# A step later, a buffer of its own, free banks ahead: three edits in a layered matmul kernel of attention and two feed-forward blocks

## The chip, the cores and the metric

The kernel runs on one core of one Trainium2 chip. The metric is the device time of one execution in microseconds (us). TensorE multiplies matrices into PSUM; VectorE and ScalarE read and write both PSUM and SBUF; GpSimd works on SBUF alone here; SyncE (SP) issues nearly all DMAs, in order. Each engine works through its own queue in order, and waits at an instruction whose operands or buffers are not ready.

## The reference

Three computations follow one another on fp32 data:

```python
out[:, :, sl] = intra + inter            # retention attention, 2 x 8 heads, 768 positions
p = domain_probs / (domain_probs.sum(-1, keepdims=True) + 1e-09)
for e in range(E):                       # mixture, 1536 tokens, 4 experts, 512 -> 1024 -> 512
    h = np.maximum(x @ w1[e], 0.0)
    out += p[:, e:e + 1] * (h @ w2[e])
h = x @ w_in                             # last block, 512 -> 2048 -> 512
g = h * (1.0 / (1.0 + np.exp(-h)))
return (g @ w_out).astype(np.float32)
```

## The kernel before, in words

**Split operands.** Every fp32 operand of a matmul is split in two parts: ScalarE copies it rounded (the high part, type fp32r), and VectorE or GpSimd subtracts that from the original (the low part). `split` does both. A product is then three matmuls: high by high, low by high, high by low.

**Four stages.** The tokens are three groups of 512. The first stage does attention for all tokens and the mixture for the first group (`gemm1`, `gemm2`, phase "a"). The second does the mixture for the other two groups together (phase "c"): seven products of halves replace eight (`pair_step`), with sums of weight quarters as left operands and sums of input quarters as right ones. The third stage (phase "b") is the last block for the first group, in 16 steps of `gemm1` and `gemm2`. The fourth (phase "d") is the last block for the other two groups, again by seven products, in both layers (`pair7` for the first layer, `down7` for the second).

**Third stage.** A step `i` runs `gemm1` of column block `i` (12 matmuls into one of four banks), the gate (ScalarE sigmoid `sg`, VectorE product, ScalarE copy `hhi`, VectorE `hlo`), and `gemm2` of block `i - 2` (12 matmuls). Every second step also needs the next weights. In an even step `split_up` makes the up weights `ua`, `ub` (ScalarE and GpSimd), and `left_out` prepares weights for the fourth stage: `left_sums` adds four quarters on GpSimd into the tile `us`, ScalarE copies its high part into `uc` (line 693), and GpSimd subtracts in place (line 694). In an odd step the parts are stored to DRAM (`wu`; `left_kept` for the split weights, line 706, and the stored function for the sums, line 700) and `split_down` makes the down weights `dh`, `dl` (ScalarE and VectorE). `combine` sums and splits the right operands for the fourth stage: a difference on VectorE (line 634), a copy on ScalarE (line 626), a subtraction on VectorE at the beginning of the next step (line 627, run by `flush`). `load(0)` and `load(1)` issue the next raw up and down weights (lines 118 and 123); each has two buffers, and the load waits until the readers of the older one are done.

**Into the fourth stage.** `left_in` loads the split weights and sums of pair 0 back from `wu` (line 711), and `left_in2` the others (line 716).

**Fourth stage.** `pair7` computes seven products into four banks `x`, `y`, `z`, `v` by the list `plan`: each entry names a product, what is emitted after it (`then`), and how many fillers follow, with a second list (`later`) after the first filler. The four banks change roles from pair to pair (`roles`). A `filler` takes a waiting second-layer block out of `fill`, and `unit` runs what is due; `after(n, fn)` makes a function due in n units. `operand` has ScalarE copy the high part (`ohi`, line 919) and returns the subtraction of the low part (`olo`, line 921). `down7(g, m, d)` is one block of six matmuls for product `ROUND[m]` and half `d`, in one of four banks `po0` to `po3` in turn. After the last two pairs (`g` = 3), the blocks of products 1, 5, 6 and 2 begin from an accumulator that ScalarE copies into the bank first (line 959), and `sums7` adds the finished blocks to other accumulators; `store` writes results out.

The order of emission is the order in each engine's queue (the schedule is written out by hand).

Of the kernel before, what the change touches and what calls it, by code (L numbers as in the profile page):

```python
# [7 lines left out]
F32 = mybir.dt.float32  # L8
F32R = mybir.dt.float32r
U32 = mybir.dt.uint32  # L10
AF = mybir.ActivationFunctionType
ALU = mybir.AluOpType
# [3 lines left out]
P = 128  # L16
# [22 lines left out]
def kernel(  # L39
# [97 lines left out]
    def load(j, n=1):  # L137
        for _ in range(n):
            if nxt[j] < len(seq[j]):
                ph, i, src = seq[j][nxt[j]]  # L140
                nxt[j] += 1
                (load_up, load_down)[j](src, i, (ph, i))
# [541 lines left out]
    def left_out(i):  # L684

        key = ("b", i)
        left_sums(key)
        low = sum_t.pop(key)
        high = leftp.tile([P, 2, 2, HW], F32R, tag="uc", name="uc").rearrange(
            "p a b n -> p (a b) n"  # L690
        )
        load(0)
        nc.scalar.activation(out=high, in_=low, func=AF.Copy)
        nc.gpsimd.tensor_tensor(
            out=low.bitcast(F32R), in0=low, in1=high.bitcast(F32), op=ALU.subtract
        )

        def stores():
            for n, t in enumerate((high.bitcast(F32), low)):
                nc.sync.dma_start(out=wu[i][:, n, 4:], in_=t)  # L700

        return stores

    def left_kept(i):
        for n, t in enumerate(up_t["b", i]):
# [18 lines left out]
    def after(n, fn):  # L724
        due.append((clock[0] + n, fn))
# [199 lines left out]
    def vadd(out, a, b, op=ALU.add, eng=nc.vector):  # L925
        eng.tensor_tensor(out=out, in0=a, in1=b, op=op)

    def acc_tile(r, d):
        if (r, d) not in acc7:
            if r in (2, 4):  # L930
                if "d" not in acc_t:
                    acc_t["d"] = accp.tile([P, KD, TW], F32, tag="acc", name="acc")
                acc7[r, d] = acc_t["d"][:, r - 2 + d]
            else:
                acc7[r, d] = tmp["d"].tile([P, TW], F32, tag=f"a{r}{d}", name=f"a{r}{d}")
        return acc7[r, d]
# [4 lines left out]

    blocks = [0]

    def down7(g, m, d, part=slice(0, TW)):

        q = 7 * g + m
        r = ROUND[m]
        po = psum.tile([P, TW], F32, tag=f"po{blocks[0] % 4}", name="po")
        blocks[0] += 1
        ops = []  # L950
        for s in range(2):
            whi, wlo = (dw_t[q][:, s, k, d * P:(d + 1) * P] for k in range(2))
            hhi, hlo = op_t[2 * g + s, r]
            ops += [(whi, hhi), (wlo, hhi), (whi, hlo)]
        a = acc_tile(r, d)
        last = g == NV // 2 - 1
        begun = last and r in (1, 5, 6, 2)
        if begun:
            nc.scalar.activation(out=po, in_=a, func=AF.Copy)
        for j, (w, h) in enumerate(ops):  # L960
            nc.tensor.matmul(  # L961
                po[:, part],
                lhsT=w,
                rhs=h[:, part],
                start=(j == 0 and not begun),
                stop=(j == len(ops) - 1),
                skip_group_check=begun,
            )

        def evacuate7():  # L970
            if begun:
                sums7(r, d, po)
            elif g == 0:
                nc.scalar.activation(out=a, in_=po, func=AF.Copy)
            else:
                vadd(a[:, part], po[:, part], a[:, part])
                if last and r == 7:
                    vadd(acc7[4, d], acc7[4, d], a, eng=nc.gpsimd)
                elif last and r == 4:
                    store(a, 2 + d, 0, part)  # L980

        due.append((clock[0] + 1, evacuate7))
        if d == 1:
            for when, fn in jobs7.pop(q, ()):
                after(when, fn)

    def sums7(r, d, po):

        a = {n: acc7[n, d] for n in ROUND}
        if r == 2:  # L990
            nc.scalar.activation(out=a[2], in_=po, func=AF.Copy)
            store(a[2], d, 0)
            return
        for n in {1: (6, 2), 5: (3, 7), 6: (4, 3, 7)}[r]:
            vadd(a[n], po, a[n])
        if r == 6:
            store(a[3], d, 1)
            store(a[7], 2 + d, 1)

# [19 lines left out]
    def pair7(i, prepare):  # L1019

        key = ("d", i)
        order = roles[0]
        x, y, z, v = (psum.tile([P, TW], F32, tag=f"ps{order[r]}", name=r) for r in "xyzv")
        roles[0] = {"x": order["z"], "y": order["x"], "z": order["v"], "v": order["y"]}
        s, low, sig = {}, {}, {}

# [10 lines left out]
        def high(r, c, eng=nc.vector):  # L1037
            low[r] = operand(i, r, c, eng)

        def times(name, c, to):  # L1040
            vadd(to, c, sig[name], ALU.mult)

        def minus(to, a, b):
            vadd(to, a, b, ALU.subtract)
# [24 lines left out]
                1,  # L1069
                [  # L1070
                    lambda: times("x", x, x),
                    lambda: high(1, x),
                    lambda: minus(sig["z"], sig["z"], x),
                ],
            ),
            (
                (4, y, False),
                [
                    lambda: low[1](),
                    lambda: minus(v, v, sig["z"]),  # L1080
                    lambda: high(5, sig["z"], nc.gpsimd),
                    lambda: low[5](),
                    lambda: high(6, v),
                    lambda: vadd(y, y, s[1]),
                    lambda: gated("y", y),
                ],
                2,
                [
# [20 lines left out]
                    for fn in later:  # L1109
                        fn()  # L1110

        def rest():
            minus(y, sig["y"], v)
            high(4, y)

        after(1, rest)
        after(2, lambda: low[4]())

    def jobs_for(key, following):

# [17 lines left out]
    with tc.manual_schedule():  # L1138
# [167 lines left out]
        tmp["sums"] = pool(sums, "sums2", side="right")  # L1306
        split_up(("b", 1), False)
        split_down(("b", 0), nc.vector)
        mixing, stores = [], []
        for i in range(nb):  # L1310
            flush()
            gemm1("b", i)
            unit()
            if i < 2:
                for _ in range(KD):
                    filler()
            elif i < nb - 2:
                gemm2("b", i - 2)
            if i % 2:
                for n in ([0, 1] if i == 1 else [i // 2 + 1]):  # L1320
                    if n < NV:
                        left_kept(n)
                stores.pop()()
                if i < nb - 1:
                    split_down(("b", (i + 1) // 2), nc.vector)
            else:
                if 2 <= i < nb - 2:
                    split_up(("b", i // 2 + 1), False)
                elif i == nb - 2:
                    left_in(0)  # L1330
                stores.append(left_out(i // 2))
            if i == 2:
                mixing = combine(acc_t["c", 0], acc_t["c", 1])
            elif i > 2:
                for job in mixing[i - 3:i - 2]:
                    job()
# [80 lines left out]
```

## Time and profile before

| what | value |
|---|---|
| median of 3 runs | 845.1 us (844.4 to 847.1) |
| profiled execution, its own time | 846.49 us |
| its span, first to last instruction | 844.7 us |
| TensorE matmuls busy | 806.8 us (96%) |
| VectorE / ScalarE / GpSimd busy | 546.7 / 351.6 / 493.0 us |
| mean granted TensorE clock | 0.98 of full speed |
| DMA, mean over the span | 145 GB/s |

The busy shares are means over stages with different limits. Matmuls are pipelined, so that the ends of their records are modelled. In rows of a timeline the columns are: start, duration, engine, line, operation, output and input tiles with their shapes, count, and in brackets the idle time of the engine before and what ended it. A row of waits has the waiting engine and line, the one waited for, the total, the number of times and the longest.

### The profile page before, as it was taken

The numbers are of one execution on the slowest core, as the hardware profiler recorded it, in microseconds if no ns is written. First come the engines' busy times: TensorE is split into PE (matmuls) and PEld (weight loads), VectorE is DVE, ScalarE is ACT, GpSimd is POOL, SyncE is SP. The second block draws the span as 40 slices with busy tenths as digits, with TensorE's granted clock in tenths as the row PEclk, the third lists the DMA queues.
The fourth block names the chain that finished last, engine by engine and source line by source line (L and its number), as shares of the span: only waits on it lengthen the run. The fifth ranks groups of instructions, "written<-read, shape, count | busy, mean of one in ns | idle before, by whom it ended". The sixth has DMA issues, their size and how long they took to land.

```text
span 844.7 us, 11026 instructions
## 1 busy us (share of the span) xinstructions
PE 806.8 (96%) x4084; PEld 660.4 (78%) x4084; DVE 546.7 (65%) x785; ACT 351.6 (42%) x602; POOL 493.0 (58%) x420
## 2 busy tenths in 40 slices
PE   8999999999999999999999999998886699999977
PEld 8888888888888888888888888886564577888766
DVE  6346586766685777777777776735335365577775
ACT  3433333343553333333333333433344367645552
POOL 3846654545675666666666667643554558675761
PEclk9999999999999999999999999999798799999999
DMA  7867768533342232232222211167455644251402
GB/s 290 308 209 242 252 225 272 184 119 122 125 134 82 97 112 87 88 113 88 91 97 98 74 52 63 55 223 264 156 169 229 225 136 139 88 180 45 162 0 100
DMA packets 39480, 122.41 MB, mean 145 GB/s; under 512 B 4434, under 2 KB 4738, under 8 KB 39426
## 3 DMA queue, kind: packets, MB, share of 16 engines
q1 hardware_dynamic: 39424, 121.70, 42.1%
q8 instruction: 32, 0.52, 0.3%
q14 instruction: 22, 0.18, 0.1%
q10 hardware_dynamic: 2, 0.00, 0.0%
HBM read 93.35 MB, written 28.34 MB: 144 GB/s over the span
## 4 chain that ended last, share of the span: by engine, by line
PE 84%; issue 4%; POOL 4%; DVE 4%; DMA 2%; ACT 2%; SPq 0%; POOLq 0%; ACTq 0%; DVEq 0%
PE po L795 21%; PE ph L532 13%; PE po L589 13%; PE y L746 11%; PE z L746 7%; PE x L746 7%; PE po L961 6%; PE s L408 2%; DMA u<-wd 1%; PE xps L447 1%; POOL ub L146 1%; POOL us L668 1%; ACT ohi L919 1%; DVE olo L921 1%; DMA ub<-wu 1%
## 5 line engine op out<-in xcount | busy, mean ns | idle before, releaser
L146 POOL TENSOR_TENSOR ub<-u,ua 128x1024 fp32r<-128x1024 f32 (+2 forms) x41 | 68.0, 1660 | 114.0 <-ACT ua L145 106.7
L795 PE MATMUL po<-hhi,dh 128*128 128x512 f32 x256 | 99.6, 389 | 0.0
L795 PE MATMUL po<-hhi,dl 128*128 128x512 f32 x256 | 99.6, 389 | 0.0
L795 PE MATMUL po<-hlo,dh 128*128 128x512 f32 x256 | 99.6, 389 | 0.0
L809 DVE TENSOR_TENSOR acc<-po,acc 128x512 f32<-128x512 f32 x120 | 79.5, 683 | 28.7 <-PE po L795 28.7
L146 POOL TENSOR_TENSOR dl<-d,dh 128x1024 fp32r<-128x1024 f32 (+1 forms) x33 | 77.0, 2334 | 12.4 <-ACT dh L145 12.4
L559 ACT ACTIVATE hhi<-ph 128x512 fp32r<-128x512 f32 x40 | 23.9, 598 | 118.0 <-DVE ph L553 85.8
L763 POOL TENSOR_TENSOR s<-s,s 128x512 f32<-128x512 f32 x32 | 48.8, 1526 | 30.9 <-ACT s L758 30.9
L532 PE MATMUL ph<-xhi,ua 128*128 128x512 f32 (+1 forms) x208 | 55.8, 391 | 9.1 <-ACT ua L145 8.4
L589 PE MATMUL po<-hhi,dh 128*128 128x512 f32 (+1 forms) x208 | 58.8, 387 | 2.2 <-ACT hhi L559 2.2
L532 PE MATMUL ph<-xhi,ub 128*128 128x512 f32 (+1 forms) x208 | 55.7, 391 | 4.4 <-POOL ub L146 4.0
L146 POOL TENSOR_TENSOR uc<-u,uc 128x512 fp32r<-128x512 f32 x16 | 20.6, 1288 | 66.9 <-ACT uc L145 66.9
L589 PE MATMUL po<-hhi,dl 128*128 128x512 f32 (+1 forms) x208 | 56.0, 373 | 0.0
L589 PE MATMUL po<-hlo,dh 128*128 128x512 f32 (+1 forms) x208 | 55.9, 372 | 0.0
L795 PEld LDWEIGHTS po<-hlo,dh 128*128 128x128 f32 x256 | 48.0, 188 | 10.0
L795 PEld LDWEIGHTS po<-hhi,dl 128*128 128x128 f32 x256 | 48.1, 188 | 10.0
L795 PEld LDWEIGHTS po<-hhi,dh 128*128 128x128 f32 x256 | 48.0, 188 | 9.9
L532 PE MATMUL ph<-xlo,ua 128*128 128x512 f32 (+1 forms) x208 | 54.7, 386 | 0.0
L532 PEld LDWEIGHTS ph<-xhi,ua 128*128 128x128 f32 x208 | 37.5, 192 | 18.6 <-ACT ua L145 10.1
L145 ACT ACTIVATE dh<-d 128x1024 fp32r<-128x1024 f32 (+2 forms) x56 | 47.0, 854 | 7.8 <-PE po L795 3.5
L532 PEld LDWEIGHTS ph<-xhi,ub 128*128 128x128 f32 x208 | 38.8, 197 | 14.1 <-POOL ub L146 6.3
L589 PEld LDWEIGHTS po<-hhi,dh 128*128 128x128 f32 x208 | 38.3, 194 | 10.9 <-ACT hhi L559 3.2
(215 smaller groups left out, 1966.4 us busy)
## 6 DMA issues: line engine op xcount, KB each, us to landing
u<-wts SPq DMA_DIRECT2D x32, 512.0 KB, 3.4
d<-wts SPq DMA_DIRECT2D x32, 512.0 KB, 3.4
words<-wts SPq DMA_DIRECT2D x32, 512.0 KB, 4.8
wd<-dec SPq DMA_DIRECT2D x32, 256.0 KB, 2.8
d<-wd SPq DMA_DIRECT2D x16, 512.0 KB, 3.6
qkt<-qk SPq DMA_DIRECT2D x12, 512.0 KB, 4.5
kvt<-kv SPq DMA_DIRECT2D x10, 512.0 KB, 4.6
ua<-wu SPq DMA_DIRECT2D x8, 640.0 KB, 5.9
```

Of the source, the lines that this page charges most:

```text
L145: nc.scalar.activation(out=hi, in_=src, func=AF.Copy)
L146: eng.tensor_tensor(out=lo, in0=src, in1=hi.bitcast(F32), op=ALU.subtract)
L408: nc.tensor.matmul(s[t, p // n][:, p % n], lhsT=qkt[r, 1, p], rhs=qkt[r, 0, p], start=True, stop=True,)
L447: nc.tensor.matmul(at, lhsT=kvt[:, 1, 2 * p + t], rhs=box[t][p], start=(c == 0), stop=(c == 0 or p >= 2),)
L532: nc.tensor.matmul(pt[:, :n], lhsT=w, rhs=x[:, k, o:o + n], start=(j == 0), stop=(j == len(ops) - 1),)
L559: nc.scalar.activation(out=hi, in_=pt, func=AF.Copy)
L589: nc.tensor.matmul(po_t[d][:, o:o + n], lhsT=w[:, d * P:(d + 1) * P], rhs=h[:, :n], start=(begin and j == 0), stop=(last and j == 2), skip ...
L746: nc.tensor.matmul(to, lhsT=a[:, k * P:(k + 1) * P], rhs=b[:, k], start=(first and j == 0), stop=(j == len(ops) - 1), skip_group_check=not ...
L763: nc.gpsimd.tensor_tensor(out=t, in0=a, in1=b, op=ALU.add)
L795: nc.tensor.matmul(po, lhsT=w, rhs=h, start=(j == 0), stop=(j == len(ops) - 1))
L809: nc.vector.tensor_tensor(out=a, in0=po, in1=a, op=ALU.add)
L961: nc.tensor.matmul(po[:, part], lhsT=w, rhs=h[:, part], start=(j == 0 and not begun), stop=(j == len(ops) - 1), skip_group_check=begun,)
```

## The change

`left_out` now emits the sums alone, ahead of `split_up`, and gives back two functions. The first, called in the next (odd) step, issues the load, makes the high part in `uc` and the low part in a tile of its own, `low`. The second, called after `split_down`, issues the two stores. In the last group of `down7` each block has a bank by the table `FINAL`; some are banks of the first layer. The copies of accumulators are emitted ahead by `begin7`: for product 1 when blocks (3, 1) and (7, 0) are issued, for 5 when the block of product 3 in the same half has been added, and for 6 and 2 when product 1 has been added. In `pair7` the subtraction from `sig["z"]` goes ahead of the copy `high(1, x)`, three more entries go from the list after product 4 to the one after product 2, two subtractions of low parts go behind the gate, and the last subtraction and copy are emitted at once instead of a unit later.

```diff
--- before.py
+++ after.py
@@ -685,21 +685,22 @@
 
         key = ("b", i)
         left_sums(key)
-        low = sum_t.pop(key)
-        high = leftp.tile([P, 2, 2, HW], F32R, tag="uc", name="uc").rearrange(
-            "p a b n -> p (a b) n"
-        )
-        load(0)
-        nc.scalar.activation(out=high, in_=low, func=AF.Copy)
-        nc.gpsimd.tensor_tensor(
-            out=low.bitcast(F32R), in0=low, in1=high.bitcast(F32), op=ALU.subtract
-        )
-
-        def stores():
-            for n, t in enumerate((high.bitcast(F32), low)):
-                nc.sync.dma_start(out=wu[i][:, n, 4:], in_=t)
-
-        return stores
+        src = sum_t.pop(key)
+
+        def halves():
+            load(0)
+            high = leftp.tile([P, 2, 2, HW], F32R, tag="uc", name="uc").rearrange(
+                "p a b n -> p (a b) n"
+            )
+            low = tmp["sums"].tile([P, 4, HW], F32R, tag="low", name="low")
+            split(nc.gpsimd, high, low, src)
+            return high, low
+
+        def stores(tiles):
+            for n, t in enumerate(tiles):
+                nc.sync.dma_start(out=wu[i][:, n, 4:], in_=t.bitcast(F32))
+
+        return halves, stores
 
     def left_kept(i):
         for n, t in enumerate(up_t["b", i]):
@@ -941,34 +942,49 @@
 
     blocks = [0]
 
+    FINAL = {3: "23", 7: "01", 1: "zx", 5: "23", 6: "01", 2: "vy", 4: "zx"}
+    begun = {}
+
+    def block_bank(last, r, d, more):
+        if last:
+            which = "2" if more else FINAL[r][d]
+            tag = f"ps{roles[1][which]}" if which in "xyzv" else f"po{which}"
+        else:
+            tag = f"po{blocks[0] % 4}"
+            blocks[0] += 1
+        return psum.tile([P, TW], F32, tag=tag, name="po")
+
+    def begin7(r, d):
+        begun[r, d] = po = block_bank(True, r, d, False)
+        nc.scalar.activation(out=po, in_=acc_tile(r, d), func=AF.Copy)
+
     def down7(g, m, d, part=slice(0, TW)):
 
         q = 7 * g + m
         r = ROUND[m]
-        po = psum.tile([P, TW], F32, tag=f"po{blocks[0] % 4}", name="po")
-        blocks[0] += 1
+        last = g == NV // 2 - 1
+        if last and (r, d) in ((3, 1), (7, 0)):
+            begin7(1, int(r == 7))
+        on = begun.pop((r, d), None)
+        po = block_bank(last, r, d, part.start > 0) if on is None else on
         ops = []
         for s in range(2):
             whi, wlo = (dw_t[q][:, s, k, d * P:(d + 1) * P] for k in range(2))
             hhi, hlo = op_t[2 * g + s, r]
             ops += [(whi, hhi), (wlo, hhi), (whi, hlo)]
-        a = acc_tile(r, d)
-        last = g == NV // 2 - 1
-        begun = last and r in (1, 5, 6, 2)
-        if begun:
-            nc.scalar.activation(out=po, in_=a, func=AF.Copy)
         for j, (w, h) in enumerate(ops):
             nc.tensor.matmul(
                 po[:, part],
                 lhsT=w,
                 rhs=h[:, part],
-                start=(j == 0 and not begun),
+                start=(j == 0 and on is None),
                 stop=(j == len(ops) - 1),
-                skip_group_check=begun,
+                skip_group_check=on is not None,
             )
+        a = acc_tile(r, d)
 
         def evacuate7():
-            if begun:
+            if on is not None:
                 sums7(r, d, po)
             elif g == 0:
                 nc.scalar.activation(out=a, in_=po, func=AF.Copy)
@@ -976,6 +992,8 @@
                 vadd(a[:, part], po[:, part], a[:, part])
                 if last and r == 7:
                     vadd(acc7[4, d], acc7[4, d], a, eng=nc.gpsimd)
+                elif last and r == 3:
+                    begin7(5, d)
                 elif last and r == 4:
                     store(a, 2 + d, 0, part)
 
@@ -993,7 +1011,10 @@
             return
         for n in {1: (6, 2), 5: (3, 7), 6: (4, 3, 7)}[r]:
             vadd(a[n], po, a[n])
-        if r == 6:
+        if r == 1:
+            begin7(6, d)
+            begin7(2, d)
+        elif r == 6:
             store(a[3], d, 1)
             store(a[7], 2 + d, 1)
 
@@ -1021,6 +1042,7 @@
         key = ("d", i)
         order = roles[0]
         x, y, z, v = (psum.tile([P, TW], F32, tag=f"ps{order[r]}", name=r) for r in "xyzv")
+        roles[1:] = [order]
         roles[0] = {"x": order["z"], "y": order["x"], "z": order["v"], "v": order["y"]}
         s, low, sig = {}, {}, {}
 
@@ -1069,20 +1091,20 @@
                 1,
                 [
                     lambda: times("x", x, x),
+                    lambda: minus(sig["z"], sig["z"], x),
                     lambda: high(1, x),
-                    lambda: minus(sig["z"], sig["z"], x),
+                    lambda: minus(v, v, sig["z"]),
+                    lambda: high(5, sig["z"], nc.gpsimd),
+                    lambda: high(6, v),
                 ],
             ),
             (
                 (4, y, False),
                 [
-                    lambda: low[1](),
-                    lambda: minus(v, v, sig["z"]),
-                    lambda: high(5, sig["z"], nc.gpsimd),
-                    lambda: low[5](),
-                    lambda: high(6, v),
                     lambda: vadd(y, y, s[1]),
                     lambda: gated("y", y),
+                    lambda: low[1](),
+                    lambda: low[5](),
                 ],
                 2,
                 [
@@ -1109,12 +1131,9 @@
                     for fn in later:
                         fn()
 
-        def rest():
-            minus(y, sig["y"], v)
-            high(4, y)
-
-        after(1, rest)
-        after(2, lambda: low[4]())
+        minus(y, sig["y"], v)
+        high(4, y)
+        after(1, lambda: low[4]())
 
     def jobs_for(key, following):
 
@@ -1306,7 +1325,7 @@
         tmp["sums"] = pool(sums, "sums2", side="right")
         split_up(("b", 1), False)
         split_down(("b", 0), nc.vector)
-        mixing, stores = [], []
+        mixing = []
         for i in range(nb):
             flush()
             gemm1("b", i)
@@ -1317,18 +1336,20 @@
             elif i < nb - 2:
                 gemm2("b", i - 2)
             if i % 2:
+                halves, stores = left
+                tiles = halves()
                 for n in ([0, 1] if i == 1 else [i // 2 + 1]):
                     if n < NV:
                         left_kept(n)
-                stores.pop()()
                 if i < nb - 1:
                     split_down(("b", (i + 1) // 2), nc.vector)
+                stores(tiles)
             else:
+                left = left_out(i // 2)
                 if 2 <= i < nb - 2:
                     split_up(("b", i // 2 + 1), False)
                 elif i == nb - 2:
                     left_in(0)
-                stores.append(left_out(i // 2))
             if i == 2:
                 mixing = combine(acc_t["c", 0], acc_t["c", 1])
             elif i > 2:
```

## Rows read from the trace of the kernel before

**Rows 1.** Waits of TensorE from 590 us to the end

```profile
PE ph L532 <- ACT ua L145: 8.4, 4, 2.5
PE po L961 <- ACT po L959: 6.0, 2, 4.8
PE ph L532 <- POOL ub L146: 4.0, 4, 1.2
PE z L746 <- DVE y L926: 2.0, 4, 0.9
```

**Rows 2.** Timeline of SP and of TensorE, 655 to 662 us

```profile
655.72 0.32 SPq L123 DMA_DIRECT2D d<-wd  x1
...
661.33 1.19 PE L746 MATMUL x<-hi,ua 128*128 128x512 f32 x2 [9.08 <-DMA ua<-wu]
```

**Rows 3.** Timeline of TensorE, third stage: passes of `gemm1`

```profile
562.83 1.07 PE L532 MATMUL ph<-xlo,ua 128*128 128x512 f32 x4
...
571.90 1.07 PE L532 MATMUL ph<-xhi,ua 128*128 128x512 f32 x4
...
577.34 1.07 PE L532 MATMUL ph<-xhi,ua 128*128 128x512 f32 x4
...
644.74 2.07 PE L532 MATMUL ph<-xhi,ub 128*128 128x512 f32 x4 [1.23 <-POOL ub L146]
```

**Rows 4.** Timeline of ScalarE, third stage, one turn of two steps

```profile
607.74 1.05 ACT L145 ACTIVATE ua<-u 128x1024 fp32r<-128x1024 f32 x1
614.12 1.06 ACT L693 ACTIVATE uc<-us 128x1024 fp32r<-128x1024 f32 x1 [5.34 <-POOL us L668]
615.09 1.04 ACT L626 ACTIVATE hi<-sum 128x1024 fp32r<-128x1024 f32 x1
...
619.38 0.60 ACT L559 ACTIVATE hhi<-ph 128x512 fp32r<-128x512 f32 x1 [2.76 <-DVE ph L566]
619.87 1.05 ACT L145 ACTIVATE dh<-d 128x1024 fp32r<-128x1024 f32 x1
...
623.96 0.60 ACT L559 ACTIVATE hhi<-ph 128x512 fp32r<-128x512 f32 x1 [2.55 <-DVE ph L566]
```

**Rows 5.** Timeline of VectorE, the same turn, and at 655 us

```profile
616.16 2.57 DVE L627 TENSOR_TENSOR lo<-sum,hi 128x1024 fp32r<-128x1024 f32 x1 [7.59 <-ACT hi L626]
...
620.95 1.23 DVE L146 TENSOR_TENSOR dl<-d,dh 128x1024 fp32r<-128x1024 f32 x1 [0.25 <-ACT dh L145]
622.09 1.22 DVE L634 TENSOR_TENSOR sum<-acc,sum 128x1024 f32<-128x1024 f32 x1
...
655.61 1.74 DVE L627 TENSOR_TENSOR lo<-sum,hi 128x1024 fp32r<-128x1024 f32 x1
```

**Rows 6.** Timeline of GpSimd, the same turn, and at 654 us

```profile
608.86 2.36 POOL L146 TENSOR_TENSOR ub<-u,ua 128x1024 fp32r<-128x1024 f32 x1 [7.93 <-ACT ua L145]
611.18 0.73 POOL L668 TENSOR_TENSOR us<-u 128x256 f32<-128x256 f32 x1
...
615.26 2.39 POOL L694 TENSOR_TENSOR us<-us,uc 128x1024 fp32r<-128x1024 f32 x1 [1.17 <-ACT uc L693]
...
654.68 1.58 POOL L668 TENSOR_TENSOR us<-us,u 128x256 f32<-128x256 f32 x1
```

**Rows 7.** DMA, 590 to 660 us: rate in 40 equal slices

```profile
GB/s 262 2 0 0 33 302 410 424 325 171 138 0 0 9 164 356 414 428 136 264 35 0 0 26 241 405 417 391 77 241 279 133 187 12 288 255 45 5 234 405
```

**Rows 8.** Waits of TensorE's weight loads, 660 to 845 us

```profile
PEld z L746 <- DVE y L926: 4.3, 6, 1.3
```

**Rows 9.** Timeline of TensorE and VectorE, last 30 us

```profile
817.09 0.69 DVE L926 TENSOR_TENSOR sg<-sg,x 128x512 f32<-128x512 f32 x1 [0.66 <-ACT ohi L919]
...
824.03 0.83 PE L961 MATMUL po<-hhi,dl 128*128 128x512 f32 x2 [4.75 <-ACT po L959]
...
840.84 0.28 PE L961 MATMUL po<-olo,dl 128*128 128x256 f32 x1
```

**Rows 10.** All DMAs that read or write `wu`, issue to landing

```profile
DMA to landing us min/median/max: 2.6/5.6/10.1
```

## Prediction

> **What bounds the kernel now.** I read the page first: TensorE is busy for 96% of the span, so a gain can only come from places where it waits, and the page's slices show these places late, in the third stage (two-layer pass over the first 512 tokens), at its end, and in the last 20 us. Then the waits of TensorE from 590 us on [rows 1]: 8.4 us for the high parts of the up weights (ScalarE's `ua`), 4.0 us for their low parts (GpSimd's `ub`), 6.0 us for ScalarE's copies of accumulators into PSUM, 2.0 us for a bank that VectorE still holds. To these comes the wait between the stages: 9.08 us for the DMA of `ua` at 661.33 [rows 2].
>
> TensorE alone needs 5.44 us a step of the third stage (571.90 to 577.34), 10.88 a turn of two steps [rows 3]. What sets the pace instead is read from one turn on three engines [rows 4 to 6]. The turn shown takes 623.96 - 607.25 = 16.71 us (607.25 being the `hhi` 0.49 before `ua`, as 619.38 stands to 619.87). It is a closed chain: `hhi` of an even step, `ua` 607.74, GpSimd `ub` 608.86 and four sums from 611.18, then `uc` at 614.12, which has stood in ScalarE's queue for the sums; behind it the copy `hi` 615.09, VectorE `lo` 616.16, the next `hhi` only at 619.38, `dh`, `dl`, a difference at 622.09, and `hhi` 623.96. From `ua` to `uc` are 6.38 us in which ScalarE could work and does not. The gate of the next step is queued behind them on ScalarE, and VectorE behind the gate. At 5.83 us too long a turn the lag eats the slack, then TensorE stops: the second pass of step 14 starts at 644.74 [rows 3], where TensorE alone would have come to it at 577.34 + 8 x 5.44 + 0.9 = 621.8. So 22.9 us are lost here.
>
> **What the change does there.** Part one: `uc` and its subtraction go behind the next step's `hhi`, and the sums go ahead of `ub` on GpSimd, so that no copy waits for sums made a moment ago. The same instructions run; none is added. What is queued on which engine in the new turn: ScalarE, `hhi`, `ua`, `hi`, gate, `hhi`, `uc`, `dh`, gate; GpSimd, four sums, `ub`, low part; VectorE, `lo`, gate, `hlo`, `dl`, difference, gate. With the start-to-start times of the rows and nothing in the way, the turn is: even step 0.49 + 0.97 (`uc` to `hi`, the same spacing as `ua` to `hi`) + 1.07 + 1.87 (difference to `hhi`) = 4.40, odd step 0.49 + 0.97 + 1.08 + 1.14 + 1.87 = 5.55, together 9.95 us, under TensorE's 10.88.
>
> Something is in the way. `lo` takes 2.57 us where `dl` of the same size takes 1.23 [rows 5]. It begins 0.90 after GpSimd's 2.39 us subtraction (615.26 to 617.65) and ends 1.08 after that one's end. The other way, a GpSimd sum takes 1.58 instead of 0.73 [rows 6] while VectorE works on two SBUF operands, and the VectorE operation behind it (655.61) again takes 1.74: they exclude one another and alternate. VectorE's gate products and `hlo`, with one operand in PSUM, are taken as free of it. The Trainium skill, "SBUF — State Buffer", section "Who interferes with whom", states this as a rule: a VectorE instruction with two SBUF inputs and a GpSimd instruction that reads SBUF lock each other out for the whole instruction. The trace agrees (2.57 for 1.23). By the rule the turn is the longer one below, without it the 9.95 above.
>
> In the old turn GpSimd was idle when `dl` and the difference ran. In the new one its low part starts just ahead of them. So I take the exclusion in full. Odd step: `uc` 0.49, low part 1.14 later and 2.39 long, then `dl` 1.08, one sum 0.65 (0.73 less its start), difference 1.08, and 0.65 to `hhi` (618.73 to 619.38): 7.48. Even step: `ua` 0.49, `ub` 1.12 later and 2.36 long, `lo` 1.08, 0.65: 5.70. Together 13.2 us a turn.
>
> Run it through. Step 3's last pass ends at 562.83 + 1.07 = 563.9 [rows 3]; 0.1 to the sigmoid, 0.6 and 0.73: `hhi` of step 3 at 565.4. Step 4: 572.9; then 13.2 each: steps 6, 8, 10, 12 at 586.1, 599.3, 612.5, 625.7. `ub` for step 14 ends 3.97 later, 629.7, against 644.74: some 15 us won of the 22.9. TensorE still waits, about a microsecond at a time for `ua` and `ub`, from step 8 on.
>
> **The end of that stage.** The load of the fourth stage's first weights (`left_in`) is issued on SP behind the stage's last `d` load, which waits for `dl`. Now it is also behind the two stores of the split sums. `hhi` of step 13 at 631.4, `dl` ended 0.49 + 1.14 + 2.39 + 1.08 later, 636.5. In the old run the weights landed 5.6 us after that `d` load was issued (655.72 to 661.33) [rows 2]; two more transfers of 512 KB ahead of them cost, at the 420 GB/s of full slices [rows 7], 2.5 us. Start of the fourth stage: 644.6, that is **16.7 us** earlier. Bounds: 9 us if the stores pace the loop (rivals), 30 if nothing is excluded. The wait before it stays some 8 us: what is late next is this load. The stores' own waits (for GpSimd's low part, done before `dl`) add nothing. The `u` loads move a step later in code, but SP issued them when the sums were done, and the sums now come earlier. The separate `low` buffer frees `us` from the store; its own reuse is a turn away.
>
> **Fourth stage, order within a pair.** The subtraction from `sg` now precedes ScalarE's copy of `x`, and the last subtraction and copy are emitted at once. No instruction is added. In the last pair VectorE waits 0.66 between the product and that subtraction [rows 9], taken to be alike in the others; the bank that `z` needs is read last by this chain, so it is free about 1.2 us sooner (0.66 plus one operation moved behind). The longest `z` wait is 0.9 [rows 1], so the waits should go: at least the 2.0 us seen on matmuls, at most the 4.3 on weight loads [rows 8]; I take **3.1**. The low part of `x` comes 0.55 later, and the next `y` needs that bank; this may cost some tenths.
>
> **The last accumulators.** Before, ScalarE copies each accumulator into the block's bank when its turn comes, behind the whole gate chain: TensorE stands 4.75 us (819.28 to 824.03) [rows 9] and 1.2 later, and after the first wait two matmuls take 0.83. Now the copies go into banks of the first layer that are free, ahead. The same number of copies (eight). The first stands in ScalarE's queue behind three operand copies and a sigmoid. The product of the last pair ends at 816.43 (0.66 before 817.09); the subtraction now follows at once and is over at some 817.05; four ScalarE operations at some 0.55 each, and the copy (0.60) ends at 819.9: TensorE waits 0.6. The second is behind two accumulator and weight copies and one operand, about 822.0: 0.8 more. The others have three blocks of cover (4.1 us) and are ready. Then eight blocks of 1.36 (a quarter of 5.44) and the last of 1.6 with its halves: 834.5 instead of 840.84 + 0.28 = 841.1. Gain **6.6**; bounds 4 (only the first wait halved) and 8. Behind the copy that waits for the first block's addition stand the operands' copies; VectorE comes to that addition just ahead of the product, so nothing is held.
>
> **Sum.** 16.7 + 3.1 + 6.6 = 26.4 us. The profiled execution took 846.49 us (span 844.7 and 1.8 around it): 820.1. It lay 1.4 above the median of the runs, 845.1, so the forecast for the median is **819**, its own range 813 to 824.
>
> **Rivals.**
> Stores pace the loop: `uc` has one buffer, and the next `uc` waits until its store has landed. From `uc` to `dl`'s end are 4.6 us, SP's `d` load and the store's issue 0.7, then the landing: 5.6 in the median [rows 10] gives 10.9 a turn, hidden under 13.2. With the longest landing, 10.1, a turn is 15.4, four turns cost 8.8 us: 828. For: six transfers of 512 KB now fall in a shorter turn. Against: `ua` and `ub` go earlier than the others. Chance 0.17.
> No exclusion counts: with 9.95 a turn TensorE is the bound, `hhi` of step 13 comes at 619.6, `dl` ends 3.6 later, the weights land 8.1 after that at 631.3, 30.0 early: 805. Against it stands `lo` at 2.57. By the skill's rule it can't happen. Chance 0.14.
> The change doesn't do what it says: the new loop closes over another wait just as long, and the tail's copies stay behind the gate chain: 845. Nothing in the queues speaks for it. Chance 0.03.
> Slower: the same store, in the third stage, landing later than any here. To lose 2.5 us after the other gains four turns must be longer by 28.9, a turn of 20.4, a landing of 15.1 us; from there the change costs. The longest seen is 10.1. Chance 0.04.
> The forecast keeps 0.62.
>
> **Numbers.** 805 to 828 takes in the forecast, the pacing stores and the unexcluded case, each at its worked time, and leaves out the last two (0.07) and the far ends of the others. Runs of this kernel differ by 0.3% (844.4 to 847.1), which is what a measurement can tell. Faster: 0.62 + 0.17 + 0.14 = 0.93; same 0.03; slower 0.04.
>
> **What would show it.** Right: turns of about 13 us between `hhi` of even steps; `dl` of some 2.6 us that ends about 1 us after GpSimd's low part; `uc` no longer waiting for sums; TensorE's waits for `ua` and `ub` shorter but there; a wait of 7 to 10 us before the fourth stage, now with two stores ahead of the load; no `z` wait above 0.3; the first of the last blocks starting within 1 us of the block before. Wrong: `uc` waiting for a DMA; turns at 10.9; a tail where the copies still stop TensorE for more than 2 us.

## The result, and the profile after

| kernel | median us (lowest to highest) | ratio to before, 95% interval |
|---|---|---|
| before | 845.11 (844.4 to 847.1) | 1 |
| changed | 819.87 (819.4 to 821.32) | 0.9701 (0.968 to 0.9721) |

The forecast of 819 us and its own range, 813 to 824, held. The profiled execution took 819.6 us, its span is 817.8, and TensorE is busy for 792.2 us of it where it was 806.8.

The waits of TensorE from 540 us on, in the changed kernel, answer to [rows 1]:

```profile
PE x L747 <- DMA ua<-wu: 12.2, 1, 12.2
PE ph L532 <- POOL ub L146: 4.5, 4, 1.3
PE x L747 <- DMA ub<-wu: 1.3, 1, 1.3
PE ph L532 <- ACT ua L145: 1.2, 3, 0.4
PE po L976 <- ACT po L959: 0.5, 1, 0.5
```

The copies into PSUM have fallen from 6.0 to 0.5 us, `ua` from 8.4 to 1.2, and the `z` waits are gone. `ub` stays. One row is longer than before: the DMA of the fourth stage's first weights, 12.2 + 1.3 us, where 9.08 stood in [rows 2].

The timeline of ScalarE, one turn (even step, odd step, next even step):

```profile
598.26 0.60 ACT L559 ACTIVATE hhi<-ph 128x512 fp32r<-128x512 f32 x1 [4.46 <-DVE ph L566]
598.75 1.05 ACT L145 ACTIVATE ua<-u 128x1024 fp32r<-128x1024 f32 x1
...
604.47 1.05 ACT L145 ACTIVATE uc<-us 128x1024 fp32r<-128x1024 f32 x1
...
611.40 0.60 ACT L559 ACTIVATE hhi<-ph 128x512 fp32r<-128x512 f32 x1 [4.45 <-DVE ph L566]
```

The turn is 611.40 - 598.26 = 13.14 us, against 16.71 before and 13.2 in the prediction. `uc` has no bracket: the sums were ready, and 5.34 us of waiting [rows 4] are gone. What fills the odd step stands in the timelines of GpSimd and of VectorE:

```profile
605.60 2.40 POOL L146 TENSOR_TENSOR low<-us,uc 128x1024 fp32r<-128x1024 f32 x1 [3.35 <-ACT uc L145]
608.08 1.60 POOL L668 TENSOR_TENSOR us<-u 128x256 f32<-128x256 f32 x1
```

```profile
606.50 2.58 DVE L146 TENSOR_TENSOR dl<-d,dh 128x1024 fp32r<-128x1024 f32 x1 [1.21 <-ACT dh L145]
609.00 1.76 DVE L634 TENSOR_TENSOR sum<-acc,sum 128x1024 f32<-128x1024 f32 x1
```

The low part ends at 608.00 and `dl` 1.08 later, though it began at 606.50 and took 1.23 alone [rows 5]. Then the sum takes 1.60 instead of 0.73, and the difference ends 1.08 after the sum. While one of the two works, the operation of the other is stretched until it ends.

The way into the fourth stage, on SP and on TensorE:

```profile
635.39 0.32 SPq L123 DMA_DIRECT2D d<-wd  x1
635.76 0.42 SPq L701 DMA_DIRECT2D wu<-uc  x1
636.28 0.38 SPq L701 DMA_DIRECT2D wu<-low  x1
636.75 1.35 SPq L712 DMA_DIRECT2D ua<-wu  x1
```

```profile
628.60 1.19 PE L532 MATMUL ph<-xhi,ub 128*128 128x512 f32 x4 [1.25 <-POOL ub L146]
...
645.63 1.19 PE L747 MATMUL x<-hi,ua 128*128 128x512 f32 x2 [12.20 <-DMA ua<-wu]
648.16 1.22 PE L747 MATMUL x<-hi,ub 128*128 128x512 f32 x2 [1.33 <-DMA ub<-wu]
...
799.20 0.73 PE L976 MATMUL po<-hhi,dl 128*128 128x512 f32 x2
...
801.38 0.73 PE L976 MATMUL po<-hhi,dl 128*128 128x512 f32 x2 [0.53 <-ACT po L959]
```

Step 14's second pass starts at 628.60, 16.1 us before the 644.74 of [rows 3]. The weights landed 645.63 - 635.39 = 10.24 us after the last `d` load was issued, where the prediction had 8.1. At the end the first of the last blocks (799.20) follows without a wait, where TensorE stood 4.75 us [rows 9], and the second waits 0.53.

**Where the time came from.** The two traces are laid side by side. The third stage's first pass starts at 538.37 instead of 539.26, and step 3 at 560.13 instead of 561.02; the same 0.9 us stand at 100 us already (100.44 and 101.36 for the same matmuls of the attention), in code that the diff does not touch, so they belong to the execution. The load of the fourth stage (first matmul with `ub`, 662.92 to 648.16) came 14.8 us earlier, 13.9 without that. From there to the last blocks (819.28 and 799.15) it was 156.36 and is 150.99: 5.4 won. From there to the last matmul's end it was 21.84 and is 14.83: 7.0 won. Together 26.3, beside 26.4 predicted; but the first two terms do not have the sizes that the prediction gave them.

### The profile page after: what moved, and what is told of

Same layout as the page of the kernel before. It is cut to its first block, busy times and chain, and to the rows that moved or that the text cites. A ratio compares the mean times of both kernels' runs of the same rounds, so it can differ in the third digit from the quotient of the medians.

```text
span 817.8 us, 11033 instructions
## 1 busy us (share of the span) xinstructions
PE 792.2 (97%) x4084; PEld 653.4 (80%) x4084; DVE 557.3 (68%) x785; ACT 349.5 (43%) x602; POOL 504.0 (62%) x420
## 4 chain that ended last, share of the span: by engine, by line
PE 84%; DVE 4%; ACT 3%; DMA 3%; POOL 3%; issue 2%; SPq 0%; ACTq 0%; POOLq 0%; DVEq 0%
PE po L796 21%; PE ph L532 13%; PE po L589 12%; PE y L747 11%; PE z L747 8%; PE x L747 8%; PE po L976 7%; DMA wu<-low 2%; PE s L408 1%; PE xps L447 1%; DVE dl L146 1%; DMA ub<-wu 1%; POOL ub L146 1%; ACT uc L145 1%; PE xps L443 1%
## 5 line engine op out<-in xcount | busy, mean ns | idle before, releaser
L532 PE MATMUL ph<-xhi,ub 128*128 128x512 f32 (+1 forms) x208 | 52.9, 376 | 4.5 <-POOL ub L146 4.5
L796 PEld LDWEIGHTS po<-hhi,dh 128*128 128x128 f32 x256 | 48.0, 188 | 9.9
L532 PE MATMUL ph<-xhi,ua 128*128 128x512 f32 (+1 forms) x208 | 53.8, 380 | 1.9 <-ACT ua L145 1.2
L532 PE MATMUL ph<-xlo,ua 128*128 128x512 f32 (+1 forms) x208 | 52.2, 372 | 0.0
L532 PEld LDWEIGHTS ph<-xhi,ub 128*128 128x128 f32 x208 | 37.0, 188 | 13.2 <-POOL ub L146 6.2
L560 DVE TENSOR_TENSOR hlo<-ph,hhi 128x512 fp32r<-128x512 f32 x40 | 27.7, 692 | 27.4 <-ACT hhi L559 27.4
```

The lines of the kernel that those rows point to most:

```text
L532: nc.tensor.matmul(pt[:, :n], lhsT=w, rhs=x[:, k, o:o + n], start=(j == 0), stop=(j == len(ops) - 1),)
L560: nc.vector.tensor_tensor(out=lo, in0=pt, in1=hi.bitcast(F32), op=ALU.subtract)
L796: nc.tensor.matmul(po, lhsT=w, rhs=h, start=(j == 0), stop=(j == len(ops) - 1))
```

## The experiments

Times are medians with the lowest and highest run; ratios are to the kernel before, in runs on the same chip.

| experiment | us | ratio, 95% interval |
|---|---|---|
| 1, sums alone | 831.17 (830.98 to 831.68) | 0.9833 (0.9819 to 0.9848) |
| 2, order alone | 839.45 (837.62 to 840.76) | 0.9929 (0.9912 to 0.9946) |
| 3, banks alone | 840.19 (839.43 to 841.05) | 0.9941 (0.9925 to 0.9958) |
| 4, down weights first | 828.16 (827.52 to 829.15) | 0.9787 (0.9772 to 0.9801) |
| 5, low part in place | 826.97 (826.37 to 827.95) | 0.9784 (0.9769 to 0.9799) |
| 6, early load | 815.63 (814.47 to 816.33) | 0.9636 (0.9622 to 0.9651) |
| 7, early load, last low part in place | 809.05 (807.95 to 809.32) | 0.9561 (0.9545 to 0.9577) |
| 8, 7 with 4 | 816.69 (815.61 to 817.3) | 0.9649 (0.9635 to 0.9663) |
| 9, 4 with the `u` load ahead | 820.63 (819.06 to 820.86) | 0.9695 (0.9679 to 0.9711) |
| 10, 7 with 9 | 808.98 (807.57 to 809.05) | 0.9559 (0.9545 to 0.9573) |
| 11, load ahead of the stores | 816.77 (816.69 to 818.33) | 0.9656 (0.9636 to 0.9676) |

**Experiments 1 to 3: each part alone.** The theory is that the three parts work in different places and add up; the rival, that one carries the gain or that they share it. Each is the kernel before with some hunks of the diff:

```diff
# 1: left_out, and its calls in the loop over the steps
+                tiles = halves()
...
+                stores(tiles)
# 2: the lists of pair7, and its end
+                    lambda: minus(sig["z"], sig["z"], x),
                     lambda: high(1, x),
...
# 3: FINAL, block_bank, begin7 and their calls
+        begun[r, d] = po = block_bank(True, r, d, False)
```

> Only the third stage's edit (sums ahead, high and low part a step later, low part in its own buffer); pair order and last blocks as before. If the three edits act apart, each in its own stretch, this has the turns of 13.2 us and the start of the fourth stage of the changed kernel (14 to 15 us earlier), with the z waits and the 4.75 us stop at the end still there: 830 to 832 us. If part of the third stage's gain only shows because the fourth stage's order changed too, it stays above 835.

> Only the order inside a pair of the fourth stage. If the z waits go and the gate chain ends some 1.2 us sooner, which also shortens the stop before the last blocks: 838 to 840 us. If the order is worth only the 2.0 us of z waits on matmuls: 842 to 844. If it does nothing by itself: 845.

> Only the last accumulators' copies, ahead and into free banks. If the stop at the end comes from where the copies stand in ScalarE's queue, the two waits of 4.75 and 1.24 us shrink to about 2 in sum: 839 to 841 us. If the gate chain itself holds the first of these blocks (its operands come no sooner), the stop stays near 4 us: 843 to 845.

All three came out inside their first ranges. Beside the 845.05 us of the kernel before in those runs, they win 13.9, 5.6 and 4.9 us, 24.4 together; the whole change wins 25.2. The waits of TensorE name the places. With the sums alone:

```profile
PE x L747 <- DMA ua<-wu: 11.8, 1, 11.8
PE po L962 <- ACT po L960: 6.0, 2, 4.8
PE ph L532 <- POOL ub L146: 4.5, 4, 1.3
PE z L747 <- DVE y L927: 2.0, 4, 0.9
```

The third stage is that of the changed kernel, and the other two waits are untouched. With the order alone the `z` waits go and the first stop at the end is shorter; with the banks alone the `z` waits stay (timelines of TensorE, first of the order, then of the banks):

```profile
816.99 1.22 PE L961 MATMUL po<-hhi,dl 128*128 128x512 f32 x2 [3.52 <-ACT po L959]
```

```profile
819.64 0.73 PE L975 MATMUL po<-hhi,dl 128*128 128x512 f32 x2 [1.55 <-ACT po L958]
```

The order thus gives 1.2 us of the end (4.75 to 3.52), which the prediction counts in its term of 6.6, and the banks need that order for the first copy to come within 1 us.

**Experiment 5: the low part in place.** The low part is again written over the sums, so that the next sums wait for its store; all else is as changed.

```diff
-            low = tmp["sums"].tile([P, 4, HW], F32R, tag="low", name="low")
+            low = src.bitcast(F32R)
```

> The changed kernel, but the low part is written over the sums again, so that the next sums wait until its store has landed. If the own buffer is needed: the store goes out 6.0 us after hhi of the odd step, lands 6.3 later, the sums take 2.9, and only then ub, lo and the gate (2.36 + 1.08 + 0.65): a turn of some 19 us against 13.2, and 838 to 848 us in all. If the later emission of the high part alone is what counts, turns of 13 to 14 us and 820 to 824.

826.97 lies between the two, so neither range held. The timeline of GpSimd shows the wait that the buffer removes:

```profile
622.66 0.74 POOL L668 TENSOR_TENSOR us<-u 128x256 f32<-128x256 f32 x1 [6.61 <-DMA wu<-us]
```

Turns are 13.8 to 15.2 us (sums at 578.82, 592.64, 607.44, 622.66, 637.07). The loop is closed on GpSimd, here from 607.44 to 622.66: sums 2.90, `ub` 2.32, low part 3.39 and the store 6.61. The expectation of 19 us had the gates and VectorE's splits in it too, which are not in this chain. So the buffer of its own is worth 7.1 us of the 25.2, and without it the store does pace the loop, the prediction's first rival, with another tile.

**Experiments 4 and 9: the down weights first.** In the odd step `dl` waits for GpSimd's low part. If the down weights are split ahead of the sums, `dl` runs while GpSimd is still without work. Theory: the turn is one `dl` shorter. Rival: the exclusion only moves.

```diff
+                if i < nb - 1:
+                    split_down(("b", (i + 1) // 2), nc.vector)
                 tiles = halves()
...
-                if i < nb - 1:
-                    split_down(("b", (i + 1) // 2), nc.vector)
```

> The changed kernel with the split of the down weights emitted ahead of the high and low part in the odd step, so that VectorE's dl comes before GpSimd's low part. If the two exclude each other: dl takes 1.23 us again instead of 2.59. If the low part then takes the port ahead of VectorE's difference, an odd half is 6.8 us instead of 7.5, a turn 12.4, and the total some 3 us less, 816 to 818; if the difference gets in first, a turn is about 11 and the total 811 to 814. If dl is long for another reason (it would still take 2.6 us), nothing changes: 819 to 821.

It was slower than the changed kernel by 7 to 8 us (8.3 by the medians, 7.3 by the ratios), which neither theory had. The timeline of VectorE answers the question that was asked:

```profile
611.64 1.23 DVE L146 TENSOR_TENSOR dl<-d,dh 128x1024 fp32r<-128x1024 f32 x1 [0.25 <-ACT dh L145]
612.78 3.42 DVE L634 TENSOR_TENSOR sum<-acc,sum 128x1024 f32<-128x1024 f32 x1
```

`dl` is back at 1.23, and the difference behind it takes 3.42 instead of 1.76: the low part (612.63, 2.48 long) now stands ahead of the difference. The odd step is 0.65 us shorter (610.06 to 616.84). The loss is elsewhere, on SP and in ScalarE's next step:

```profile
612.89 0.32 SPq L123 DMA_DIRECT2D d<-wd  x1
613.30 0.38 SPq L118 DMA_DIRECT2D u<-wd  x1
```

```profile
604.83 1.06 ACT L145 ACTIVATE ua<-u 128x1024 fp32r<-128x1024 f32 x1 [2.46 <-DMA u<-wd]
```

The `u` load is emitted in `halves`, which now comes behind `split_down`; so it stands behind the `d` load, which waits for `dl`, and `ua` waits for its data. Experiment 9 changes this alone:

```diff
+                load(0)
                 if i < nb - 1:
                     split_down(("b", (i + 1) // 2), nc.vector)
...
         def halves():
-            load(0)
```

> The experiment with the down weights split first, and now the load of the next raw up weights emitted ahead of the load of the raw down weights on SP. Theory (the time was lost because the up load stood behind the down load on SP, so that `ua` waited 1.4 to 2.5 us for its DMA): these waits vanish, the odd step stays at the 6.8 us that it took there (610.06 to 616.84) and the even step returns to the 5.7 of the changed kernel, a turn of 12.5 us instead of 13.15; four turns win 2.6 us, of which the later store of the low part gives back about 0.6: 817 to 819. Rival (the longer turn comes from the exclusion of VectorE and GpSimd in the new order, and the wait for the DMA only fills the gap): turns stay at 14 to 15 us and the time at 826 to 829.

These us are back (820.63, where 828.16 was) and `ua` no longer waits for its data, so the place of that load in SP's queue was the cause. The range of 817 to 819 was missed: there is no gain on the changed kernel. The turn is 617.13 - 604.14 = 12.99 us, within 0.2 of the changed kernel's. The odd step keeps its 6.78, but the even step is 6.21 instead of 5.7. Rows of ScalarE, GpSimd and VectorE show the new chain:

```profile
604.14 0.60 ACT L559 ACTIVATE hhi<-ph 128x512 fp32r<-128x512 f32 x1 [3.26 <-DVE ph L566]
...
610.92 0.60 ACT L559 ACTIVATE hhi<-ph 128x512 fp32r<-128x512 f32 x1 [3.80 <-DVE ph L566]
611.42 1.05 ACT L145 ACTIVATE ua<-u 128x1024 fp32r<-128x1024 f32 x1
...
617.13 0.60 ACT L559 ACTIVATE hhi<-ph 128x512 fp32r<-128x512 f32 x1 [3.23 <-DVE ph L566]
```

```profile
606.71 2.49 POOL L146 TENSOR_TENSOR low<-us,uc 128x1024 fp32r<-128x1024 f32 x1 [4.29 <-ACT uc L145]
...
613.04 2.37 POOL L146 TENSOR_TENSOR ub<-u,ua 128x1024 fp32r<-128x1024 f32 x1
```

```profile
613.45 3.04 DVE L627 TENSOR_TENSOR lo<-sum,hi 128x1024 fp32r<-128x1024 f32 x1 [1.20 <-ACT hi L626]
```

The low part starts 0.9 us later than in the changed kernel, measured from `hhi` (2.57 against 1.63), GpSimd works on without a break through the sums to `ub`, and `lo` waits for that. 2.57 to the low part, 8.70 to `ub`'s end at 615.41, 1.08 to `lo`'s, 0.65 to `hhi`: 13.0. Of the 0.65 us that `dl` won in the odd step, `lo` gave back 0.5 in the even one. So the theory was right about the load, and the rival's reason, the exclusion that moves, is why the turn wins almost nothing. What is won at the end of the stage goes on SP: the last `d` load is issued 2.4 us earlier than in the changed kernel (633.02 against 635.39), but the load of `ua` now stands behind four stores instead of two, and TensorE gets it at 645.80 against 645.63.

The Trainium skill, "SBUF — State Buffer", section "Who interferes with whom", gives the lock between a VectorE instruction with two SBUF inputs and a GpSimd instruction that reads SBUF as one for the whole instruction. The traces agree: `dl` takes 1.23 us beside an idle GpSimd (experiment 4) and 2.58 beside a running one (the changed kernel), in kernels that differ in the order alone.

**Experiments 6, 7 and 11: the load of the fourth stage's first weights.** The changed kernel still waits 13.5 us here. In 11 `left_in(0)` goes ahead of the two stores of step 13; in 6 it goes to the beginning of that step, ahead of its `d` load as well; 7 is 6 with the last low part in place.

```diff
# 11
+                if i == nb - 3:
+                    left_in(0)
                 stores(tiles)
# 6
             gemm1("b", i)
+            if i == nb - 3:
+                left_in(0)
# 7, beside the edit of 6
-            low = tmp["sums"].tile([P, 4, HW], F32R, tag="low", name="low")
+            low = src.bitcast(F32R)
+            if i < NV - 1:
+                low = tmp["sums"].tile([P, 4, HW], F32R, tag="low", name="low")
```

> The changed kernel, with the load of the fourth stage's first weights issued on SP between the last `d` load and the two stores of step 13 instead of behind those stores. It prices the two stores that stand ahead of that load. Theory of the prediction's sum (they cost their bytes, 2.5 us): `ua` lands 7.7 us after the `d` load is issued and the fourth stage starts some 2.5 us earlier than the 645.6 of the changed kernel, at about 643.1. Rival (they cost the whole difference between 10.2 us now and 5.6 us in the kernel before): 5.6 us after the `d` load, a start at 641.0. Second rival (it is not the stores but the time of day, other transfers in flight): the start stays at 645 or later. What the time wins is at most this, 815 to 817, less what the first copy of `x` then waits for the later store of the low part, up to all of it.

> The changed kernel with the load of the fourth stage's first weights issued right behind gemm1 of step 13, not behind the d load and the two stores. If that queue place is the whole of the 12.2 us wait, it goes, and 808 to 810 us result. If the next thing late is the fourth stage's first copy on ScalarE, which writes where the low part of the sums lay and waits until its last store has landed (650.7 in the changed kernel), the products x, y and z start early but the next one waits: 4 us won, 815 to 817.

> As the run with the early load, and the last low part alone is written over its sums, so that no tile of the fourth stage lies where a store is still reading. The first copy then waits only for ScalarE's own high part of the sums (about 642): 12 us won, 807 to 810. If the first copy's wait for the store did not matter, the same as the run with the early load alone.

Experiment 11 prices the stores (TensorE):

```profile
641.79 1.19 PE L747 MATMUL x<-hi,ua 128*128 128x512 f32 x2 [8.43 <-DMA ua<-wu]
643.32 1.22 PE L747 MATMUL x<-hi,ub 128*128 128x512 f32 x2 [0.33 <-DMA ub<-wu]
```

The `d` load went out at 635.32, so `ua` landed 6.5 us behind it, against 10.24: the two stores cost 3.8 us on `ua`, 4.8 with the wait for `ub`, where the prediction has 2.5. The time fell by 3.1 us (3.8 by the ratios), since ScalarE's first copy of `x` then comes at 651.85 and TensorE stands 2.0 us behind it. That copy follows the issue of the last store of `low` (648.37) by 3.5 us, as it does in experiment 6 (645.09 to 648.54); its bracket names another DMA, so that the store is its cause is read from this distance alone. TensorE's wait is larger in experiment 6. There the weights are ready when the third stage ends, and the stop moves into the fourth (ScalarE, then TensorE):

```profile
648.54 0.60 ACT L1051 ACTIVATE s<-x 128x512 f32<-128x512 f32 x1 [6.01 <-DMA wu<-low]
```

```profile
649.68 1.22 PE L747 MATMUL y<-hi,ua 128*128 128x512 f32 x2 [7.19 <-ACT s L1051]
```

`s` is a tile of the fourth stage and lies where `low` lay, so it waits until the last low part is stored. In the changed kernel the same wait exists (7.69 us at 650.78 on ScalarE), hidden behind the late weights. Experiment 7 takes away its cause, and the wait with it: 809.05 us, where `y` waits 1.32. It beats both kernels; the changed one by 1.4% of the time before (0.9561 against 0.9701).

**Experiments 8 and 10: both ideas together.** 8 is 7 with the edit of experiment 4, 10 is 7 with that of experiment 9.

> Early load, last low part in place, and the down weights split first. If these act apart: 3 us less than the run before it, 804 to 807. If the fourth stage's start is set by the stores' landing alone, no less than the run before.

> The fastest kernel so far (first weights of the fourth stage loaded a step earlier, last low part in place, 809.05 us) with the down weights split first and the up load ahead of the down load on SP. Theory (order of the two loads on SP cost the 8 us of the run that combined them): turns of 12.5 us give back about 2.6 us of waits before step 14, less what the fourth stage then waits for its first weights: 806 to 808.5. Rival (the split order itself costs the time): 815 to 818, as in the run that combined them.

8 missed its 804 to 807: it lost 7.6 us on 7, as 4 lost on the changed kernel, and the load's place on SP brings them back in 10: the same cause. 10 equals 7, a miss by little: the fourth stage starts at 631.85 instead of 634.56, but then stands at `y` (TensorE of 10, then of 7):

```profile
642.17 1.12 PE L748 MATMUL y<-hi,ua 128*128 128x512 f32 x2 [2.14 <-ACT s L1052]
```

```profile
643.12 0.72 PE L749 MATMUL y<-hi,ua 128*128 128x512 f32 x2 [1.32 <-ACT s L1053]
```

The copies `s` are queued behind the last `uc`, which waits for the store of the one before (to 639.88 and 640.71). That this is what caps both was not tried. Of the 2.7 us by which 10 starts the stage earlier, 0.95 are left at `y` and 0.4 at the last blocks (786.99 against 787.38). Behind its stop the mean granted clock of 10 is 0.57 from 642 to 646 us, and the pair at `y` takes 1.12; in 7 the clock is 1.00 there, and the pair takes 0.72.

## Why the prediction was right, and where it was not

**The turn of the third stage.** 13.14 against 13.2 predicted, built as it said: `dl` 2.58 long ending 1.08 after the low part, one sum, and the difference 1.08 after that. The end of `ub` for step 14 was forecast at 629.7 and the pass behind it started at 628.60, or 629.5 without the 0.9 us by which this execution started earlier. Experiments 4 and 9 show the cause, the exclusion: where `dl` comes before GpSimd's low part, it takes 1.23 again, and the next operation of VectorE is the long one (3.42).

**The end of that stage** is the term of the sum that was mis-sized. `dl` ends at 635.36, 636.3 on the old clock of events, where 636.5 was forecast. From there the load was put at 8.1 us, two stores at the full rate of 420 GB/s; it took 10.24, and the second half of the weights cost another 0.9 of waiting. The wait became 13.5 us, where the prediction had some 8 and gave 7 to 10 as a sign of being right; besides these 3.0 us, TensorE was done with the third stage at 633.43, 634.3 on the old clock, and not at the 636.6 that 644.6 less 8 implies. The term was 13.9, by the traces and by experiment 1, instead of **16.7**. Experiment 11 shows the main cause: the two stores alone cost 4.8 and not 2.5. With no store ahead of it `ua` still takes 6.5 us there, and not 5.6 as in the kernel before; why stays open. (The lower bound of that term, 9, is a slip: 16.7 less the 8.8 of the pacing stores is 7.9.)

**The order in the pairs** was given **3.1** with bounds of 2.0 and 4.3, and the stretch won 5.4, out of its bounds. 0.7 of it lies in the first pair (662.92 to 683.12 before, 648.16 to 667.69 now), and the runs don't show these as the order's: that pair takes 20.00 us with the order alone and 19.90 with the banks alone, against 20.20. The 4.7 behind that are alike with the order alone (131.46 and 131.40 us against 136.16). That is about the waits of the weight loads [rows 8], 4.3, and some tenths: the upper bound, not the middle, was nearer the price. The 2.0 us of waits of the matmuls alone under-count here; that the rest is the weight loads' waiting fits the numbers and was not tried apart. The tenths feared for the low part of `x` don't show.

**The last accumulators**: 7.0 against **6.6**, with the first block free of waiting, the second at 0.53 where 0.8 was forecast, and the others without a wait.

**The sum** was good to 1 us by luck: two errors, 2.8 too much at the end of the third stage and 2.3 too little in the pairs, met. The own range, 813 to 824, held the time by the bounds of the terms and not by each term.

**Rivals.** The stores did not pace the loop: `uc` waits for no DMA until the last one (1.81 us at 642.04), when the gates are over. There the last `low` waits too, 5.64 us for the store of the one before it (644.61): the reuse that the prediction put a turn away. The unexcluded case fell with `dl` at 2.58. The slower case and no effect fell with the result. What no step had was the wait of `s` on the last store of `low`; it cost nothing here, and 6.6 us (815.63 against 809.05) as soon as the load came earlier.

## What to carry to other kernels

Emit an operation where its operands have long been made, and count for every instruction so moved what it takes along: the `u` load that moved behind a waiting `d` load cost 8 us, more than the edit was to win. When two engines exclude one another, add their times in the loop, and look where the lock falls next before reordering; and price a load by what is issued ahead of it. A wait hidden behind a longer one becomes the bound when that one goes, so the trace of the changed kernel is worth reading for waits that cost nothing yet.

## What the runs showed that was not expected

The two engines take turns where both have work queued: in four places of three kernels, VectorE's operation ends 1.08 or 1.09 us after GpSimd's (608.00 and 609.08, 609.68 and 610.76 in the changed kernel, 615.11 and 616.20 in experiment 4, 615.41 and 616.49 in experiment 9), and of two VectorE operations the one that meets the low part is stretched most (`dl` 2.58 and the difference 1.76 in the changed kernel, 1.23 and 3.42 in experiment 4).

Here a load on SP's queue pays for the stores ahead of it more than their bytes. Behind the `d` load and no store `ua` landed after 6.5 us (experiment 11), behind two stores of 512 KB after 10.24, behind four after 12.8 (experiment 9, 633.02 to 645.80; 13.0 in experiment 4): 1.9 and then 1.3 us for each, where 512 KB at 420 GB/s make 1.25. SP itself was held too: the issue of `ua` took 1.35 us behind the stores and 0.38 ahead of them. Why the first two cost more stays open.

The stop before the fourth stage costs more than its length. Granted clock and TensorE's work in the changed kernel, by stretches:

```profile
630.00:636.00 6.00, 3.44 (x16) 1.00 0.12 47
636.00:642.00 6.00, 0.00 (x0) 0.65 0.94 242
642.00:646.00 4.00, 0.37 (x1) 0.50 0.99 329
646.00:650.00 4.00, 2.67 (x6) 0.50 0.71 290
650.00:654.00 4.00, 4.00 (x16) 0.83 0.89 214
```

The columns are the stretch, its length, TensorE's busy time and rows, the granted clock, the DMA share and GB/s. After 12 us without work the clock is at 0.50, its lower level of 1.2 GHz, and the first matmuls take 1.19 a pair; in experiment 7, which does not stop there, they take 0.61 at a clock of 1.00.
